# The first chunk's attention in plain float32 products over its three key blocks

## The chip, the cores and the metric

One core of a Trainium2 chip runs the kernel. The time is the device time of one execution in microseconds. The kernel before was timed three times: 816.13, 816.46 and 816.73 us, median 816.46 us. One further execution was profiled; it took 815.83 us, of which 814.1 us lie between its first and its last instruction (the span).

## The reference

Attention with a few sink keys and a sliding window, then a two-layer network on the concatenated heads. The shapes are batch 4, 8 heads, 768 positions, head size 64; 4 sinks, window 128; model width 512, hidden width 2048; all float32.

```python
scores = scale * np.matmul(q, k.transpose(0, 1, 3, 2))
keep = is_sink | in_window
scores = np.where(keep, scores, -1000000000.0)
scores = scores - np.max(scores, axis=-1, keepdims=True)
a = np.exp(scores)
a = a / (np.sum(a, axis=-1, keepdims=True) + 1e-09)
x = np.matmul(a, v)          # then heads side by side: 3072 x 512
h = x @ w_in
r = np.maximum(h, 0.0)
out = (s * (r * r) + b) @ w_out
```

## The kernel before, in words

**Chunks.** The 3072 rows are cut into eight chunks of 384 rows (half a sequence). A chunk has an attention part and a network part (`moe_steps`). The attention of chunk 0 runs by itself at the start; from then on the network steps of chunk c are issued together with the attention slots of chunk c+1. The instructions of each engine then run in a fixed order that the scheduling framework wrote when the kernel was built; an instruction whose operand is late holds up everything behind it on its engine.

**High and low parts.** TensorE is fed with float32r operands, a rounded form of float32. To keep precision, an operand is split into a high part (its rounded value) and a low part (what is left), and a product is made of two or three products of parts that add up in PSUM. Making parts is work for ScalarE (the rounding copy), VectorE and GpSimd (the subtraction).

**Attention, a head at a time, three units of 128 rows (i = 0, 1, 2).** `prep_head` (L225 to L239) splits queries, keys and values. `unit_a` multiplies queries with 144 or 272 keys (the 16 first keys as sinks, and the one or two blocks of 128 keys that the window reaches) in two products (L253, L254), applies the mask and the row maximum on VectorE in one instruction (L258, tile sm), takes the exponential on ScalarE (L264), and copies the sink columns aside on GpSimd (L265). `unit_b` transposes the block or two blocks on TensorE (L273, L275) and splits the result (L277 on ScalarE, L278 on VectorE, tile hl). `unit_c` multiplies with the values (L302). The row sums are collected in zz, and their reciprocal and the sinks' share are applied once for a pair of heads through further small products (L314, L325, L327; L284 to L288, L328 to L331).

**Weights.** Both weight matrices are cut into 32 pieces of 128x512, 8 bytes for a value (they come as float64). `load_piece` fetches a piece raw (512 KB) into the buffer w{p+2} of 32 named buffers w0 to w31, the last two pieces elsewhere. `make_piece` turns it into high and low parts: two ScalarE passes (L160, L161), two VectorE passes (L162, tile wt; L163, tile wraw), one GpSimd add (L165), two steps later a ScalarE rounding copy (L169), another two steps later the low part (L174, on VectorE for three pieces in four, otherwise on GpSimd), into buffer w{p}. Network step f of the first chunk needs pieces 2f and 2f+1; they are kept for the other seven chunks.

**Network.** `l1(f)` makes 12 products 128x384 (L379), Relu on ScalarE (L382), r on VectorE (L383), g high on ScalarE (L385), g low on VectorE (L386). `l2(f)` makes 9 products 128x512 (L397). There are 16 steps f in a chunk.

**The two stages of the start.** The text calls *first stage* the time up to the first L383 of chunk 0, and *second stage* the time from there to the fourteenth L383 of chunk 0; by then all pieces but a last one have been through VectorE.

## Time and profile before

| | |
|---|---|
| median of three runs | 816.46 us |
| the profiled execution | 815.83 us, span 814.1 us |
| TensorE matmul busy | 767.5 us, 94% of the span |
| VectorE (DVE) busy | 534.5 us, 66% |
| ScalarE (ACT) busy | 517.2 us, 64% |
| GpSimd (POOL) busy | 294.1 us, 36% |
| mean granted TensorE clock | 0.952 of full speed |

TensorE is the busiest engine over the whole, but not everywhere: a view that cuts the span into stretches shows which engine has no idle time in each. A row of such a view gives the stretch, then for each engine the busy time and, in brackets, the number of instructions, then the granted clock, the share of the DMA engines and their rate. In a timeline, a row gives the start, the duration, the engine, the line, the operation and its tiles, and in square brackets the idle time before it and what ended it. In a view of groups, a row gives the line, the engine, the operation, its tiles and shapes, the count, then busy us and the mean in ns, then the idle time before.

### The profile page before, as it was taken

What the parts mean: (1) busy time and instruction counts of PE and PEld (TensorE: products, weight loads), DVE (VectorE), ACT (ScalarE), POOL (GpSimd) and SP (SyncE); (2) the same over time, 40 slices, a digit from 0 to 9 for tenths busy, and PEclk for the clock granted to TensorE, in tenths of its full rate; (3) what the DMA queues carried; (4) which work ended last, traced back from release to release, by engine and by line L of the source; (5) the groups of instructions that cost most, each with busy time, mean ns of one, the idle gap of its engine ahead of it and who ended that gap; (6) DMA issues with size and microseconds to landing.
All of it is one profiled execution on the core that took longest, in us unless ns stands there. A gap on an engine that the chain in (4) does not pass through costs nothing.

```text
span 814.1 us, 12959 instructions
## 1 busy us (share of the span) xinstructions
PE 767.5 (94%) x4304; PEld 698.8 (86%) x4304; DVE 534.5 (66%) x1301; ACT 517.2 (64%) x1306; POOL 294.1 (36%) x473
## 2 busy tenths in 40 slices
...
GB/s 205 223 260 286 111 29 38 46 67 73 47 49 41 56 77 41 65 45 52 52 44 54 69 52 50 55 43 52 52 45 54 74 54 47 28 1 39 1 0 43
DMA packets 31754, 55.44 MB, mean 68 GB/s; under 512 B 4032, under 2 KB 18368, under 8 KB 31680
## 3 DMA queue, kind: packets, MB, share of 16 engines
...
## 4 chain that ended last, share of the span: by engine, by line
PE 79%; DVE 12%; ACT 3%; issue 2%; POOL 1%; DMA 1%; SPq 0%; POOLq 0%; ACTq 0%; DVEq 0%
PE h L379 31%; PE po L397 30%; PE o L302 7%; PE sc L254 3%; PE sc L253 2%; PE tp L273 2%; DVE wt L162 2%; PE tp L275 2%; DVE wraw L163 2%; DVE r L383 2%; DVE sm L258 1%; PE ts L314 1%; DVE w L174 1%; DVE g L386 1%; PE os L325 1%
## 5 line engine op out<-in xcount | busy, mean ns | idle before, releaser
L379 PE MATMUL h<-x,w 128*128 128x384 f32 x1536 | 303.9, 348 | 8.6 <-DVE negm L258 5.4
L397 PE MATMUL po<-w,g 128*128 128x512 f32 x1152 | 294.7, 400 | 1.4 <-DVE g L386 1.4
L379 PEld LDWEIGHTS h<-x,w 128*128 128x128 f32 x1536 | 274.2, 193 | 13.4 <-DVE negm L258 6.8
L397 PEld LDWEIGHTS po<-w,g 128*128 128x128 f32 x1152 | 209.1, 188 | 42.7 <-DVE g L386 1.8
L258 DVE CUSTOM_DVE_ANT_0 sm<-sc,msk 128x272 f32<-128x272 f32 (+1 forms) x192 | 79.8, 416 | 103.2 <-PE sc L254 75.0
L265 POOL COPY psk<-sm 128x48 f32<-128x48 f32 x192 | 56.7, 296 | 226.2 <-ACT sm L264 225.4
L382 ACT ACTIVATE r<-h 128x384 f32<-128x384 f32 x128 | 63.0, 492 | 115.5 <-PE h L379 114.4
L302 PE MATMUL o<-hl,vv 128*128 128x128 f32 x704 | 124.3, 296 | 2.7 <-DVE hl L278 2.5
L383 DVE SCALAR_TENSOR_TENSOR r<-r,sb 128x384 f32<-128x384 f32 x128 | 83.6, 654 | 56.3 <-ACT r L382 56.3
L264 ACT ACTIVATE sm<-sm,negm 128x272 f32<-128x272 f32 (+1 forms) x192 | 97.2, 506 | 29.3 <-DVE negm L258 28.2
L386 DVE SCALAR_TENSOR_TENSOR g<-r,sb,g 128x384 fp32r<-128x384 f32 x128 | 83.7, 655 | 44.3 <-ACT g L385 41.8
L302 PEld LDWEIGHTS o<-hl,vv 128*128 128x128 f32 x704 | 104.1, 206 | 4.7 <-DVE hl L278 3.8
L233 POOL TENSOR_TENSOR kl<-kraw,kh 128x416 fp32r<-128x416 f32 (+1 forms) x64 | 81.8, 1278 | 54.2 <-ACT kh L231 53.0
L385 ACT ACTIVATE g<-r,sb 128x384 fp32r<-128x384 f32 x128 | 78.8, 616 | 35.0 <-DVE r L383 33.0
L277 ACT CAST hl<-tp 128x256 fp32r<-128x256 f32 (+1 forms) x192 | 67.2, 351 | 33.5 <-PE tp L275 32.5
L278 DVE TENSOR_TENSOR hl<-tp,hl 128x256 fp32r<-128x256 f32 (+1 forms) x192 | 76.0, 397 | 10.8 <-ACT hl L277 7.9
L238 POOL TENSOR_TENSOR vv<-vraw,vv 128x192 fp32r<-128x192 f32 (+1 forms) x64 | 46.4, 726 | 77.6 <-ACT vv L237 77.2
L273 PE MATMUL tp<-identr,sm 128*128 128x128 f32 x192 | 56.5, 295 | 10.0 <-ACT sm L264 5.7
L253 PE MATMUL sc<-kh,qs 128*128 128x272 f32 (+1 forms) x192 | 58.4, 306 | 5.7 <-ACT kh L231 3.4
L254 PE MATMUL sc<-kl,qs 128*128 128x272 f32 (+1 forms) x192 | 58.4, 306 | 3.6 <-POOL kl L233 3.5
L310 DVE TENSOR_TENSOR xm<-o,y 64x384 f32<-64x384 f32 x64 | 35.4, 553 | 24.9 <-ACT y L309 24.5
L232 DVE TENSOR_TENSOR qs<-qraw,qs 64x384 fp32r<-64x384 f32 x64 | 43.5, 680 | 8.0 <-ACT qs L228 5.9
...
## 6 DMA issues: line engine op xcount, KB each, us to landing
wraw<-in_w SPq DMA_DIRECT2D x32, 512.0 KB, 5.6
...
```

What stands on the lines that cost most here:

```text
L233: nc.gpsimd.tensor_tensor(out=hd.kl[:, :kw], in0=hd.k[:, :kw], in1=hd.kh[:, :kw].bitcast(F32), op=ALU.subtract)
L253: nc.tensor.matmul(sc[:, :n], hd.qs[:, qs], hd.kh[:, c0:c0 + n], start=True, stop=False)
L254: nc.tensor.matmul(sc[:, :n], hd.qs[:, qs], hd.kl[:, c0:c0 + n], start=False, stop=True)
L258: nc.vector.tensor_tensor_reduce(out=sm[:, :n], in0=sc[:, :n], in1=m, scale=-0.125, scalar=BIG, op0=ALU.add, op1=ALU.min, accum_out=negm[: ...
L264: nc.scalar.activation(sm[:, :n], sm[:, :n], AF.Exp, bias=negm[:, uu], scale=-1.0, accum_out=pp.zz[:, i, hh:hh + 1])
L278: nc.vector.tensor_tensor(out=hl[:, 1, :n], in0=tp[:, :n], in1=hl[:, 0, :n].bitcast(F32), op=ALU.subtract)
L302: nc.tensor.matmul(hd.o[:, qs], hd.vv[:, cur - j, :], hl[:, t, j * P:(j + 1) * P], start=((j, t) == mm[0]), stop=((j, t) == mm[-1]))
L379: nc.tensor.matmul(h[:, :CH], pieces[2 * f][:, wi, cc * P:(cc + 1) * P], x[xi][:, cc, :], start=(i == 0), stop=(i == 11))
L383: nc.vector.scalar_tensor_tensor(out=r, in0=r, scalar=s_ap, in1=r, op0=ALU.mult, op1=ALU.mult)
L385: nc.scalar.activation(gg[:, 0, :], r, AF.Identity, bias=b_ap, scale=1.0)
L386: nc.vector.scalar_tensor_tensor(out=gg[:, 1, :], in0=r, scalar=b_ap, in1=gg[:, 0, :].bitcast(F32), op0=ALU.add, op1=ALU.subtract)
L397: nc.tensor.matmul(po[tb], gg[:, gi, tsl], pieces[2 * f + 1][:, wi, :], start=(f == 0 and i == 0), stop=(f == NF - 1 and i == 2))
```

## The change

For chunk 0 alone, the attention slots come from a new function, `first_slots`.

- No parts are made of queries, keys, values or weights of the attention. A product of float32 operands is asked of TensorE directly. Queries of a pair of heads are loaded into a buffer whose other 64 partitions are set to zero, so that one product works on 128 partitions.
- Unit i multiplies with all i+1 key blocks up to its own (128, 256 or 384 keys), under full masks that hold window and sinks together (`m_full`, six blocks of 128 made in `constants`). The sinks need no path of their own: no copies to psk, no sink products, no row-sum products for the pair.
- The row sum is inverted for each unit and applied on VectorE to the exponentials (three small or middle VectorE instructions), before the transposes.
- Transposes are 1, 2 and 3 blocks; the copy out of PSUM is on ScalarE for i = 0 and 1 and on VectorE for i = 2. The three units of a head share three products with the values, of 384, 256 and 128 columns, once for a head.
- The result's high part is taken on ScalarE, its low part on VectorE (on GpSimd before).
- Buffers: queries, keys and values of the four pairs lie in w16 to w23, the transposed exponentials in w24 to w27, the scores in two buffers w28 and w29, the masks in w30 (warm was and is in w31). A raw piece p goes into w{p+2}: pieces 14 to 28 find their buffer used by the first chunk's attention.
- All loads of chunk 0, 28 transfers, are asked for ahead of the first piece of the weights.

The attention of chunks 1 to 7, the network and the preparation of a piece are not edited.

```diff
--- before.py
+++ after.py
@@ -57,6 +57,18 @@
     msk = const.tile([P, 3 * W + P + NS], MDT, tag="msk", name="msk")
     m_1, m_odd, m_even = (msk[:, j * W:(j + 1) * W] for j in range(3))
     m_0 = msk[:, 3 * W:]
+
+
+    def late(j, shape, dtype, name):
+        n = 1
+        for x in shape[1:]:
+            n *= x
+        t = const.tile([P, 2 * DM], F32, tag=f"w{j}", name=name)
+        t = t if dtype is F32 else t.bitcast(dtype)
+        return t
+
+    m_all = late(2 * NF - 2, [P], MDT, "m_all")
+    m_full = [m_all[:, a * P:(a + j + 1) * P] for j, a in ((0, 0), (1, 1), (2, 3))]
 
 
 
@@ -110,7 +122,7 @@
 
 
         nc.vector.scalar_tensor_tensor(out=low, in0=rel, scalar=w_ap, in1=low, op0=ALU.is_lt, op1=ALU.mult)
-        nc.vector.tensor_scalar(out=snk[:, :NS], in0=kix[:, :NS], scalar1=n_ap, scalar2=None, op0=ALU.is_lt)
+        nc.vector.tensor_scalar(out=snk, in0=kix, scalar1=n_ap, scalar2=None, op0=ALU.is_lt)
         nc.vector.tensor_tensor(out=tmp[:, :NS], in0=low[:, :NS], in1=snk[:, :NS], op=ALU.mult)
         nc.vector.tensor_tensor(out=tmp[:, :NS], in0=snk[:, :NS], in1=tmp[:, :NS], op=ALU.subtract)
 
@@ -127,6 +139,19 @@
         mask(m_1[:, P:2 * P], low)
         mask(m_1[:, 2 * P:], tm2[:, :NS])
         mask(m_even[:, P:P + NS], snk[:, :NS])
+
+        for j in range(BLK):
+            mj = m_full[j]
+            for kb in range(j + 1):
+                keep = low if kb == j else upp if kb == j - 1 else None
+                if kb > 0:
+                    kept = keep
+                elif keep is None:
+                    kept = snk
+                else:
+                    kept = (tmp, tm2)[j]
+                    nc.vector.tensor_tensor(out=kept, in0=keep, in1=snk, op=ALU.max)
+                mask(mj[:, kb * P:(kb + 1) * P], kept)
         cp = nc.gpsimd.tensor_copy
         cp(out=m_even[:, :P], in_=m_1[:, :P])
         cp(out=m_even[:, P + NS:], in_=m_1[:, P:2 * P])
@@ -345,13 +370,8 @@
         def slot(t):
             def f():
 
-                for j, (fn, a) in enumerate(ahead.get(t, ())):
+                for fn, a in ahead.get(t, ()):
                     fn(k, a)
-                    if k.c == 0 and t == 0 and j == 0:
-                        constants()
-                if k.c == 0 and t == 0:
-                    nc.sync.dma_start(sb[:, 0:1], s.partition_broadcast(P))
-                    nc.sync.dma_start(sb[:, 1:2], b.partition_broadcast(P))
                 if t < n:
                     unit_a(k, *units[t])
                 if 0 <= t - LB < n:
@@ -363,6 +383,94 @@
             return f
 
         return k, [slot(t) for t in range(n + LC + LD)]
+
+
+    def first_slots():
+        k = new_chunk(0)
+        F0 = 2 * NF - 16
+        cc, tt, hd_o = {}, {}, {}
+
+        def load(pr):
+            pp = k.pairs[pr] = Chunk()
+            qk = const.tile([P, 2, DM], F32, tag=f"w{F0 + 2 * pr}", name="q_0")
+            kv = const.tile([P, 2, DM], F32, tag=f"w{F0 + 2 * pr + 1}", name="kv_0")
+
+            nc.gpsimd.memset(qk[D:, 0, :CH], 0.0)
+            nc.gpsimd.memset(qk[:D, 1, :CH], 0.0)
+            for hh in range(2):
+                hs = slice(hh * D, (hh + 1) * D)
+                nc.sync.dma_start(qk[hs, hh, :CH], qT[0, pr, hs, :CH])
+                h = 2 * pr + hh
+                nc.sync.dma_start(kv[hs, 0, :2 * P], kT[0, h, hs, NS:NS + 2 * P])
+                nc.sync.dma_start(kv[hs, 0, 2 * P:CH], kT[0, h, hs, 2 * NS + 2 * P:2 * NS + 3 * P])
+            nc.sync.dma_start(kv[:, 1, :CH].rearrange("p (n e) -> p n e", n=BLK),
+                              v[0, pr, :, :BLK].rearrange("p n h d -> p n (h d)"))
+            pp.q, pp.k, pp.v = qk[:, :, :CH], kv[:, 0, :CH], kv[:, 1, :CH]
+
+        def fa(h, i):
+            pp = k.pairs[h // 2]
+            n = (i + 1) * P
+            u = h * BLK + i
+            uu = slice(u, u + 1)
+            sc = ps("sc0")
+            nc.tensor.matmul(sc[:, :n], pp.q[:, h % 2, i * P:(i + 1) * P], pp.k[:, :n], start=True, stop=True)
+            sm = const.tile([P, CH], F32, tag=f"w{F0 + 12 + u % 2}", name="sm0")
+            nc.vector.tensor_tensor_reduce(out=sm[:, :n], in0=sc[:, :n], in1=m_full[i], scale=-0.125, scalar=BIG,
+                                           op0=ALU.add, op1=ALU.min, accum_out=negm[:, uu])
+            z = wk.tile([P, 3], F32, name="z0", tag="zr", bufs=2)
+            nc.scalar.activation(sm[:, :n], sm[:, :n], AF.Exp, bias=negm[:, uu], scale=-1.0, accum_out=z[:, 0:1])
+            nc.vector.tensor_scalar(out=z[:, 1:2], in0=z[:, 0:1], scalar1=1e-9, scalar2=None, op0=ALU.add)
+            nc.vector.reciprocal(out=z[:, 2:3], in_=z[:, 1:2])
+            nc.vector.tensor_scalar(out=sm[:, :n], in0=sm[:, :n], scalar1=z[:, 2:3], scalar2=None, op0=ALU.mult)
+            cc[(h, i)] = sm
+
+        def fb(h, i):
+            sm = cc.pop((h, i))
+            if i == 0:
+                tt[h] = const.tile([P, 4, 2 * P], F32, tag=f"w{F0 + 8 + h % 4}", name="tt0")
+            tp = ps("tp0")
+            for kb in range(i + 1):
+                nc.tensor.transpose(tp[:, kb * P:(kb + 1) * P], sm[:, kb * P:(kb + 1) * P], ident)
+
+            t0, c0 = i // 2, i % 2 * P
+            out = tt[h][:, t0:t0 + i + 1, c0:c0 + P]
+            (nc.scalar.copy if i < 2 else nc.vector.tensor_copy)(out, tp[:, :(i + 1) * P].rearrange("p (k c) -> p k c", c=P))
+
+        def fc(h, i):
+            if i < BLK - 1:
+                return
+            pr, hs = h // 2, slice(h % 2 * D, (h % 2 + 1) * D)
+            pp = k.pairs[pr]
+            o = ps("o0")
+            t = tt.pop(h).rearrange("p k c -> p (k c)")
+            for kb in range(BLK):
+                c0 = kb * 3 * P
+                nc.tensor.matmul(o[:, kb * P:CH], pp.v[:, kb * P:(kb + 1) * P], t[:, c0:c0 + (BLK - kb) * P],
+                                 start=(kb == 0), stop=(kb == BLK - 1))
+            nc.scalar.copy(k.x[0][hs, pr, :], o[hs, :CH])
+            nc.vector.tensor_tensor(out=k.x[1][hs, pr, :], in0=o[hs, :CH], in1=k.x[0][hs, pr, :].bitcast(F32), op=ALU.subtract)
+
+        units = [(h, i) for h in range(H) for i in range(BLK)]
+        n = len(units)
+
+        def slot(t):
+            def f():
+                if t == 0:
+                    for pr in range(H // 2):
+                        load(pr)
+                        if pr == 0:
+                            constants()
+                    nc.sync.dma_start(sb[:, 0:1], s.partition_broadcast(P))
+                    nc.sync.dma_start(sb[:, 1:2], b.partition_broadcast(P))
+                if t < n:
+                    fa(*units[t])
+                if 0 <= t - 1 < n:
+                    fb(*units[t - 1])
+                if 0 <= t - 3 < n:
+                    fc(*units[t - 3])
+            return f
+
+        return k, [slot(t) for t in range(n + 3)]
 
 
     def moe_steps(x, store, wk, before=None, last=False):
@@ -508,7 +616,7 @@
         weights(2 * f + 3 + LOADS, 2 * f + 3)
 
     NC_ = 2 * B
-    k, slots = attn_slots(0)
+    k, slots = first_slots()
     for f in slots:
         f()
     one = const.tile([P, 1], F32, tag="one", name="one")
```

What the edits do to the order of the engines is seen at three places. A line number of the changed kernel differs from that of the kernel before: L383 (r) is L491 there, L162, L163 and L174 are L187, L188 and L199, L258 (sm) of later chunks is L283, L149 (the raw load) is L174.

**VectorE at the first r of the network.** Before (L162, L163, L174: the three passes of a piece; L329: the end of a pair's attention; L258 is already chunk 1):

```order
L329 TENSOR_TENSOR xm<-zb,xm 128x384
L258 ISA sm,negm<-sc,msk 128x272
L258 ISA negm 128x1
L232 TENSOR_TENSOR qs<-qraw,qs 64x384
L162 TENSOR_SCALAR wt<-wraw 128x512
L174 TENSOR_TENSOR w_981<-wraw,w_981 128x512
L163 SCALAR_TENSOR_TENSOR wraw<-wraw,wt 128x512
L162 TENSOR_SCALAR wt<-wraw 128x512
L258 ISA sm,negm<-sc,msk 128x272
L258 ISA negm 128x1
L383 SCALAR_TENSOR_TENSOR r<-r,sb 128x384 x2
```

After (L451: the low part of a head's attention result; L437: the copy of the transposed block for i = 2):

```order
L437 COPY tt_530<-tp_553 128x3x128
L199 TENSOR_TENSOR w_1149<-wraw,w_1149 128x512
L187 TENSOR_SCALAR wt<-wraw 128x512 x2
L188 SCALAR_TENSOR_TENSOR wraw<-wraw,wt 128x512 x2
L451 TENSOR_TENSOR x_0_97<-o_558,x_0_96 64x384
L199 TENSOR_TENSOR w_1242<-wraw,w_1242 128x512
L187 TENSOR_SCALAR wt<-wraw 128x512
L283 ISA sm,negm<-sc,msk 128x272
L283 ISA negm 128x1
L188 SCALAR_TENSOR_TENSOR wraw<-wraw,wt 128x512
L491 SCALAR_TENSOR_TENSOR r<-r,sb 128x384
```

Ahead of the first r there stood 10 instructions of L162, 9 of L163 and 6 of L174; now there stand 21, 21 and 13 of the same three passes. Up to the fourteenth r it was 32, 32 and 23, and is 32, 32 and 24: eleven pieces have moved from the second stage into the first.

**The queue of SyncE at its start.** Before (raw pieces in between the first loads; sb: the two scalars):

```order
L80 DMA lim<-in_n_sink 128x2
L81 DMA lim<-in_window 128x2
L195 DMA qraw<-in_qT 128x384
L197 DMA vraw<-in_v 128x384
L210 DMA kraw<-in_kT 128x416
L217 DMA vsraw<-in_vsk 128x128
L353 DMA sb<-in_s 128x1
L354 DMA sb<-in_b 128x1
L149 DMA wraw<-in_w 128x1024 x2
```

After (kv and q: keys, values and queries of the last pair of chunk 0):

```order
L404 DMA kv_184<-in_kT 64x256
L405 DMA kv_184<-in_kT 64x128
L406 DMA kv_184<-in_v 128x384
L463 DMA sb<-in_s 128x1
L464 DMA sb<-in_b 128x1
L174 DMA wraw<-in_w 128x1024 x11
L220 DMA qraw<-in_qT 128x384
```

Behind the two loads of lim (the limits), four loads and the two scalars stood ahead of the first raw piece; now all 28 loads of chunk 0 and the two scalars stand there, and then eleven pieces follow one upon the other.

**TensorE about the fourth head of chunk 0.** Before (two products of scores a unit, transposes, products with the values of 128 columns):

```order
L275 MATMUL tp<-identr,sm 128x128
L254 MATMUL sc<-kl,qs 128x144
L302 MATMUL o<-hl,vv 128x128 x2
L314 MATMUL ts<-identr,psk_89 128x128 x3
L253 MATMUL sc<-kh,qs 128x272
L254 MATMUL sc<-kl,qs 128x272
L273 MATMUL tp<-identr,sm 128x128
L275 MATMUL tp<-identr,sm 128x128
L302 MATMUL o<-hl,vv 128x128 x6
L325 MATMUL os<-xsk,vs 128x384
L327 MATMUL zb<-xsk,sel 128x384
L253 MATMUL sc<-kh,qs 128x272
```

After:

```order
L416 MATMUL sc_323<-kv_162,q_161 128x128
L433 MATMUL tp_332<-identr,sm_306 128x128 x3
L416 MATMUL sc_337<-kv_162,q_161 128x256
L433 MATMUL tp_347<-identr,sm_325 128x128
L416 MATMUL sc_350<-kv_162,q_161 128x384
L433 MATMUL tp_359<-identr,sm_339 128x128 x2
L448 MATMUL o_363<-tt_300,kv_162 128x384
L448 MATMUL o_363<-tt_300,kv_162 128x256
L448 MATMUL o_363<-tt_300,kv_162 128x128
L416 MATMUL sc_369<-kv_173,q_172 128x128
L433 MATMUL tp_378<-identr,sm_352 128x128 x3
```

A head had 6 products of scores, 5 transposes and 10 products with the values, and for a pair of heads 5 more; now it has 3, 6 and 3, with operands in plain float32, and the three products of one head with the values stand together, ahead of the next head's third group of transposes.

## The prediction

> **What bounds the kernel now.** The first view cuts the span into three stretches: up to the first r, from there to the fourteenth, and about a chunk's length after that.
>
> ```profile
> core 0: us, PE busy (x) PEld busy (x) DVE busy (x) ACT busy (x) POOL busy (x), PEclk, DMA share, GB/s
> 0.00:75.00 75.00, 56.38 (x236) 47.42 (x237) 58.62 (x172) 59.23 (x157) 47.58 (x85) 0.64 0.72 235
> 75.00:176.00 101.00, 80.13 (x415) 70.98 (x414) 97.04 (x181) 82.80 (x189) 67.72 (x71) 0.90 0.24 77
> 182.00:272.00 90.00, 89.95 (x531) 82.84 (x530) 59.45 (x156) 58.44 (x158) 29.23 (x55) 1.00 0.18 51
> ```
>
> From 182 us TensorE has no idle time and its full clock; the edit touches nothing there. In the second stage VectorE is busy for 97.04 of 101 us (96%): it sets the pace. In the first stage nothing is full (VectorE 78%, ScalarE 79%, TensorE 75% at a granted clock of 0.64): the engines wait for one another. The stages' ends are read in VectorE's timeline (the middle row is an r that nothing held up).
>
> ```profile
> 74.94 2.62 DVE L383 SCALAR_TENSOR_TENSOR r<-r,sb 128x384 f32<-128x384 f32 x2
> 79.95 0.61 DVE L383 SCALAR_TENSOR_TENSOR r<-r,sb 128x384 f32<-128x384 f32 x1
> 176.11 0.92 DVE L383 SCALAR_TENSOR_TENSOR r<-r,sb 128x384 f32<-128x384 f32 x1
> ```
>
> What fills VectorE is read in its groups, first those of the second stage:
>
> ```profile
> L163 DVE SCALAR_TENSOR_TENSOR wraw<-wraw,wt 128x512 int32<-128x512 int32 x23 | 19.7, 856 | 0.2
> L162 DVE TENSOR_SCALAR wt<-wraw 128x512 int32<-128x512 int32 x22 | 15.2, 691 | 1.4 <-ACT wraw L161 1.4
> L174 DVE TENSOR_TENSOR w<-wraw,w 128x512 fp32r<-128x512 f32 x17 | 12.4, 728 | 0.0
> L386 DVE SCALAR_TENSOR_TENSOR g<-r,sb,g 128x384 fp32r<-128x384 f32 x12 | 12.2, 1024 | 0.1
> L383 DVE SCALAR_TENSOR_TENSOR r<-r,sb 128x384 f32<-128x384 f32 x13 | 12.1, 935 | 0.0
> ```
>
> Nearly half of the stage, 47.3 us, is the preparation of weights (first three rows). So the time is set by how much VectorE work lies ahead of the fourteenth r, plus VectorE's idle time up to there. At that point the old and the new order stand equal (all pieces through), and I take the rest as unchanged. The change in time is then that of the first stage plus that of the second.
>
> **Second stage.** By the order, 11 of L162, 12 of L163 and 6 of L174 leave it. Recorded durations overlap by some 0.07 us (below, the 0.43 us row at 12.91 is followed at 13.27), so what leaves is 11 x 0.62 + 12 x 0.79 + 6 x 0.66 = 20.2 us of 97.0. A dozen GpSimd adds leave too, and with them a part of what VectorE waits for GpSimd: r lasts 0.935 us here on the mean and 0.61 undisturbed, g's low part (L386, the same shape) 1.024: 9 us of excess in the two rows. GpSimd's 67.72 us fall by some 13, a fifth, so 2 us. Left: 74.8 us, at 96% 78 us. TensorE comes close: its 415 matmuls would take 415/531 x 90 = 70 us at the pace of the third stretch, at this stage's clock of 0.90 78 us. Two engines near their limit in fixed orders also wait for each other: I take 80 us, **21 us less**. Bounds: 78 us (VectorE alone) and 88 us (each adds 10 us of waits to TensorE's 78).
>
> **First stage, its start.** The rows of the constants, of SyncE's first issues and of the first landing:
>
> ```profile
> 0.75 0.39 SPq L80 DMA_DIRECT2D lim<-in_n_sink  x1
> 4.50 0.91 SPq L149 DMA_DIRECT2D wraw<-in_w  x2
> 6.50 0.16 DVE L515 TENSOR_SCALAR one<-wp 128x1 f32<-128x1 f32 x1
> 9.09 0.52 DVE L99 TENSOR_SCALAR sc<-sc 128x128 f32<-128x128 f32 x1
> 10.07 0.21 DVE L101 TENSOR_SCALAR sc<-sc 128x128 f32<-128x128 f32 x1
> 11.28 0.68 ACT L160 ACTIVATE wraw<-wraw 128x512 int32<-128x512 uint32 x1 [2.77 <-DMA wraw<-in_w]
> 12.05 0.72 DVE L119 TENSOR_SCALAR msk<-sc 128x16 bf16<-128x16 f32 x5
> 12.69 0.30 DVE L258 CUSTOM_DVE_ANT_0 sm<-sc,msk 128x144 f32<-128x144 f32 x1
> 12.91 0.43 DVE L258 CUSTOM_DVE_ANT_0 sm<-sc,msk 128x272 f32<-128x272 f32 x1
> 13.27 0.43 DVE L258 CUSTOM_DVE_ANT_0 sm<-sc,msk 128x272 f32<-128x272 f32 x1
> 14.09 0.53 ACT L264 ACTIVATE sm<-sm,negm 128x272 f32<-128x272 f32 x1
> ```
>
> The masks no longer queue behind a split of queries, so they start at 6.6 in place of 9.09, take the 3.6 us of before and 1.4 us more (six blocks at 0.13, two maxima at 0.23 like the sm of 144 columns, a wider comparison): the first scores are masked at 11.5 us. Eight issues took 3.75 us, so 32 ahead of the first piece take 15 us: it is asked for at 15.8 in place of 4.50. The median landing of a piece takes 5.6 us:
>
> ```profile
> wraw<-in_w SPq DMA_DIRECT2D x32, 512.0 KB, 5.6
> ```
>
> With two ScalarE passes at 0.55 start to start VectorE gets it at 22.5 us. Until then it has only units: a pair of units, with two score buffers, costs 0.7 for sm, 1.0 for two exponentials, some 0.5 for the three new VectorE steps, 0.8 for transposes and the next scores, 3 us; six units, 9 us, bring it to 20.5. So nothing is lost by the late start that the units don't fill, but 2 us; a raw piece later than 22.5 costs its lateness.
>
> **First stage, the rest.** From 22.5 us the order gives VectorE 18 units, 21 pieces through L162 and L163, 13 through L174, two splits of queries and one sm of chunk 1. The prices:
>
> ```profile
> L163 DVE SCALAR_TENSOR_TENSOR wraw<-wraw,wt 128x512 int32<-128x512 int32 x9 | 8.2, 907 | 0.1
> L232 DVE TENSOR_TENSOR qs<-qraw,qs 64x384 fp32r<-64x384 f32 x10 | 6.9, 694 | 2.8 <-ACT qs L228 2.3
> L162 DVE TENSOR_SCALAR wt<-wraw 128x512 int32<-128x512 int32 x10 | 5.5, 558 | 0.1
> L310 DVE TENSOR_TENSOR xm<-o,y 64x384 f32<-64x384 f32 x8 | 4.4, 552 | 0.3
> L174 DVE TENSOR_TENSOR w<-wraw,w 128x512 fp32r<-128x512 f32 x6 | 4.1, 684 | 0.0
> L328 DVE TENSOR_TENSOR xm<-os,xm 128x384 f32<-128x384 f32 x4 | 2.2, 558 | 1.3 <-PE os L325 1.3
> L285 DVE RECIPROCAL zr<-zr 128x6 f32<-128x6 f32 x4 | 0.7, 185 | 0.1
> 54.63 0.42 DVE L162 TENSOR_SCALAR wt<-wraw 128x512 int32<-128x512 int32 x1
> ```
>
> Pieces, each less 0.07: 21 x (0.49 + 0.84) + 13 x 0.61 = 35.8 us. A head: sm of 128, 256 and 384 columns by the rows of 144 and 272, 0.21 + 0.34 + 0.47; three additions like L515, 0.27; three reciprocals, 0.35; the scaling, 0.21 us at 128 columns (L101) and 0.42 at 512 (L162 undisturbed), so 0.14 + 0.21 + 0.28; the copy of 384 columns out of PSUM like L328, 0.49; the low part like L310, 0.48. That is 3.24 us, six heads 19.4 us. The rest 1.6 us. Sum 56.8 us.
>
> The new additions and scalings are of L162's kind, which GpSimd holds up: 0.558 us on the mean here and 0.42 undisturbed. At 0.14 us each, 36 of them cost 5.0 us; the bounds are nothing and the rival below. With 61.8 us of work VectorE runs at 78% (the first stage so far) to 96% (the second). I take 94%, near the second, because pieces now stand between the units in its queue: 65.7 us. The first r comes at 88.2 us, **13.2 us later** than at 75. Bounds: 56.8/0.96, first r at 81.7 (6.7 later); 61.8/0.78, at 101.7 (26.7 later).
>
> **TensorE in the first stage.** How long a plain float32 product streams, no row shows; the last product of the kernel is one, with a single column:
>
> ```profile
> L538 PEld LDWEIGHTS cnt<-one,bad x2: 79/80/82, 807.4 to 807.4; 128*1 128x1 f32 x2
> L538 PE MATMUL cnt<-one,bad x2: 163/164/164, 807.4 to 807.4; 128*1 128x1 f32 x2
> 25.22 0.52 PE L253 MATMUL sc<-kh,qs 128*128 128x272 f32 x1
> 25.54 0.43 PE L254 MATMUL sc<-kl,qs 128*128 128x272 f32 x1
> 25.77 0.41 PE L273 MATMUL tp<-identr,sm 128*128 128x128 f32 x1
> 25.98 0.42 PE L275 MATMUL tp<-identr,sm 128*128 128x128 f32 x1
> ```
>
> It is recorded as two weight loads and two matmuls. So the low bound is two passes; the high bound is four, since two operands of two parts have four products of parts. A head has 2 x (128 + 256 + 384) = 1536 columns of products. At half clock 272 columns take 0.23 us (25.54 to 25.77), new weights 0.09 more, a transpose 0.21: two passes give 2.6 + 1.1 + 1.3 = 5.0 us a head, four 7.6; eight heads 40 or 61 us. I take four. From 11.5 us that ends at 73, and copy, low part, twelve products of h and Relu add some 6: 79 us, short of VectorE's 88. VectorE is the cover for these 21 us; without it they would lie on the path.
>
> The Trainium skill (FP8 and Floating Point Precision, TensorE Precision Notes) says that true float32 takes four passes through the array; by it the head costs the 7.6 us, and the sum stays.
>
> **The rivals.** *More is won.* GpSimd loses the splits of keys and values and the sink copies of chunk 0, so it may hold up nothing: both low bounds, 6.7 - 23 = -16 us, 800 us. Against it: the exposed instructions have grown in number.
>
> *TensorE takes the second stage over.* 88 us there, 13.2 - 13 = 0, 816 us. For it: the two engines' sums are equal, 78 us.
>
> *GpSimd's adds hold VectorE up in full* (the side of slower). Every L163 releases an add on GpSimd, and what follows it on VectorE now is mostly of the exposed kind.
>
> ```profile
> L165 POOL TENSOR_TENSOR wraw<-wraw 128x512 int32<-128x512 int32 x7 | 7.6, 1085 | 2.9 <-DVE wraw L163 2.9
> L286 DVE CAST zh<-zr x7: 163/514/1037, 23.9 to 154.2; 128x6 fp32r<-128x6 f32 x7
> ```
>
> A copy of six elements took 163 ns alone and 1037 at worst. If each of 21 adds blocks VectorE for its 1.085 us, that is 22.8 us where I have counted 8 (5.0 and the 0.14 in L162): 15 us more, -8 + 15 = +7, 823 us. It decides from 0.37 us an add on beyond what is counted. Against it: L162 itself lost only 0.14.
>
> The Trainium skill (SBUF — State Buffer, SBUF: two separate sides) says that the port pair which the two engines share is an exclusive lock, held for a whole instruction, which is this rival; the 1037 ns agree with it, the mean of L162 shows it seldom in full.
>
> *TensorE at half clock, unit after unit.* If it stands still while a pair of units is exponentiated and scaled (1.7 us, twelve pairs, 20 us) and the clock stays at 0.5, the first stage is 11.5 + 61 + 20 + 6 = 99 us, 24 - 21 = +3, 819 us. For it: the granted clock was 0.64 in that stage. Against it: four-pass products keep TensorE denser than now.
>
> **How the numbers follow.** Forecast: 13.2 - 21 = -7.8 us on the profiled execution's own 815.83, 808.0; the median of the runs is 0.6 higher, so 808.7. Chances: the forecast (803 to 814) 0.44, more won 0.17, TensorE in the second stage 0.11, GpSimd 0.15, half clock 0.13. The range, 799 to 822, takes in the forecast, the second stage's rival and half clock, and about half of each of the other two, whose own spread goes some us to either side: 0.16 is left out. What this kernel's measurement can tell from no change is about 0.2%, 1.6 us: faster 0.41 + 0.17 + 0.04 = 0.62, same 0.08, slower 0.30.
>
> **What would show it.** Right: r number one at 82 to 93 us, number fourteen 77 to 84 us later; VectorE over 90% busy from 22 us on; each plain product as two matmuls, columns at a quarter of float32r's rate; the first piece at VectorE near 22 us. Wrong: long idle rows on VectorE ended by TensorE or by a weight transfer in the first stage; additions and scalings of over 0.5 us on the mean (GpSimd); a granted clock of 0.5 all through; a second stage above 88 us with VectorE below 90%.

## The result and the profile after

The changed kernel takes 827.01 us (median of four runs, 826.80 to 827.62), the kernel before, timed beside it, 816.56 us (816.13 to 816.73). The ratio is 1.0135, with an interval of 1.0123 to 1.0148: slower by 10.5 us, where 8 us faster was forecast. The profiled execution has a span of 825.8 us.

The loss is all made by the sixteenth r of chunk 0. From the start of that r to the end of the span it is 625.9 us before (814.1 - 188.23) and 625.3 us after (825.8 - 200.55); in all kernels of this study it lies between 624.2 and 626.5 us. So a kernel's time here is the moment of its sixteenth r and a nearly constant rest.

First the stretches of the kernel before, cut at 25.75 us, the first, the eighth and the sixteenth r, and at last the whole up to the sixteenth (columns as in the prediction's first fence):

```profile
0.00:25.75 25.75, 13.70 (x48) 8.54 (x49) 17.73 (x58) 16.62 (x42) 16.11 (x36) 0.73 0.61 205
25.75:74.94 49.19, 42.63 (x188) 38.82 (x188) 40.84 (x116) 42.55 (x115) 31.41 (x49) 0.59 0.77 251
74.94:123.50 48.56, 37.97 (x198) 33.67 (x197) 45.68 (x86) 39.62 (x93) 32.29 (x35) 0.89 0.31 104
123.50:188.23 64.73, 54.01 (x288) 47.92 (x287) 61.17 (x119) 51.18 (x118) 44.11 (x46) 0.92 0.17 54
0.00:188.23 188.23, 148.31 (x717) 128.95 (x718) 165.41 (x373) 149.97 (x365) 123.92 (x165) 0.80 0.43 139
```

The same stretches of the changed kernel:

```profile
0.00:25.75 25.75, 15.79 (x48) 8.92 (x48) 11.90 (x64) 7.39 (x21) 7.60 (x25) 0.73 0.52 141
25.75:97.77 72.02, 44.05 (x135) 28.36 (x136) 65.71 (x165) 56.29 (x129) 36.47 (x31) 0.67 0.66 228
97.77:148.03 50.26, 39.48 (x198) 33.68 (x198) 46.35 (x87) 36.43 (x86) 30.95 (x32) 0.86 0.10 29
148.03:200.55 52.52, 49.19 (x294) 44.87 (x294) 37.16 (x91) 34.67 (x89) 21.32 (x33) 1.00 0.24 70
0.00:200.55 200.55, 148.52 (x672) 115.82 (x673) 161.12 (x401) 134.78 (x321) 96.34 (x121) 0.81 0.39 126
```

Up to the sixteenth r VectorE works 161.1 us where it worked 165.4, 4.3 us less, and is idle 39.4 us where it was idle 22.8. Stretch by stretch its idle time changes by +5.8 (8.0 to 13.9, the start), -2.0, +1.0 and +11.8 us (3.6 to 15.4, from the eighth to the sixteenth r). In that last stretch TensorE is busy 49.19 of 52.52 us at full clock: there it is the limit, and VectorE has run out of work.

In VectorE's timeline the ends of the two stages, the first and the fourteenth r:

```profile
97.77 0.61 DVE L491 SCALAR_TENSOR_TENSOR r<-r,sb 128x384 f32<-128x384 f32 x1
189.09 0.62 DVE L491 SCALAR_TENSOR_TENSOR r<-r,sb 128x384 f32<-128x384 f32 x1
```

The first stage takes 22.8 us more (forecast 13.2), the second 91.3 us in place of 101.2, 9.9 less (forecast 21). VectorE's groups between 25.75 and 97.77 us:

```profile
L188 DVE SCALAR_TENSOR_TENSOR wraw<-wraw,wt 128x512 int32<-128x512 int32 x21 | 17.3, 829 | 0.0
L187 DVE TENSOR_SCALAR wt<-wraw 128x512 int32<-128x512 int32 x21 | 12.3, 595 | 4.3 <-ACT wraw L186 4.3
L199 DVE TENSOR_TENSOR w<-wraw,w 128x512 fp32r<-128x512 f32 x13 | 12.1, 931 | 0.0
L424 DVE TENSOR_SCALAR sm<-sm,z 128x128 f32<-128x128 f32 (+2 forms) x18 | 9.9, 552 | 0.0
...
L422 DVE TENSOR_SCALAR z<-z 128x1 f32<-128x1 f32 x18 | 2.6, 145 | 1.2 <-ACT sm L421 1.0
```

The first three rows are weight preparation, 41.7 of 65.7 us. With VectorE at 91% of this stretch, the first stage looks like VectorE's. The experiments show that the amount of its work is not what sets the pace.

### The profile page after: what moved, and what is told of

Same layout as the page of the kernel before. It is cut to its first block, busy times and chain, and to the rows that moved or that the text cites. A ratio compares the mean times of both kernels' runs of the same rounds, so it can differ in the third digit from the quotient of the medians.

```text
span 825.8 us, 12816 instructions
## 1 busy us (share of the span) xinstructions
PE 767.0 (93%) x4260; PEld 685.6 (83%) x4260; DVE 530.5 (64%) x1329; ACT 500.6 (61%) x1262; POOL 267.2 (32%) x429
## 4 chain that ended last, share of the span: by engine, by line
PE 81%; DVE 9%; ACT 3%; SPq 2%; issue 2%; DMA 2%; POOL 1%; POOLq 0%; DVEq 0%; ACTq 0%
PE h L487 31%; PE po L505 30%; PE o L327 7%; PE sc L279 2%; PE sc L278 2%; PE tp L298 2%; PE o L448 2%; PE tp L300 2%; DMA wraw<-in_w 2%; DVE w L199 1%; DVE wt L187 1%; DVE wraw L188 1%; PE ts L339 1%; DVE sm L424 1%; PE os L350 1%
## 5 line engine op out<-in xcount | busy, mean ns | idle before, releaser
L283 DVE CUSTOM_DVE_ANT_0 sm<-sc,msk 128x272 f32<-128x272 f32 (+1 forms) x168 | 70.6, 420 | 101.9 <-PE sc L279 75.4
L491 DVE SCALAR_TENSOR_TENSOR r<-r,sb 128x384 f32<-128x384 f32 x128 | 81.7, 638 | 60.6 <-ACT r L490 60.6
L327 PE MATMUL o<-hl,vv 128*128 128x128 f32 x624 | 101.3, 282 | 2.1 <-DVE xm L335 1.1
L289 ACT ACTIVATE sm<-sm,negm 128x272 f32<-128x272 f32 (+1 forms) x168 | 85.3, 508 | 26.4 <-DVE negm L283 25.4
L258 POOL TENSOR_TENSOR kl<-kraw,kh 128x544 fp32r<-128x544 f32 (+1 forms) x56 | 70.7, 1263 | 53.0 <-ACT kh L256 53.0
L327 PEld LDWEIGHTS o<-hl,vv 128*128 128x128 f32 x624 | 83.8, 191 | 3.4 <-DVE xm L335 1.6
L303 DVE TENSOR_TENSOR hl<-tp,hl 128x256 fp32r<-128x256 f32 (+1 forms) x168 | 67.3, 400 | 10.4 <-ACT hl L302 7.7
L263 POOL TENSOR_TENSOR vv<-vraw,vv 128x256 fp32r<-128x256 f32 (+1 forms) x56 | 38.5, 687 | 86.0 <-ACT vv L262 83.9
L190 POOL TENSOR_TENSOR wraw<-wraw 128x512 int32<-128x512 int32 x32 | 38.6, 1211 | 53.9 <-ACT wraw L185 17.4
L278 PE MATMUL sc<-kh,qs 128*128 128x272 f32 (+1 forms) x168 | 47.3, 281 | 2.2 <-DVE hl L303 1.5
L279 PE MATMUL sc<-kl,qs 128*128 128x272 f32 (+1 forms) x168 | 48.3, 287 | 0.0
L298 PE MATMUL tp<-identr,sm 128*128 128x128 f32 x168 | 46.2, 275 | 2.1 <-DVE negm L283 1.0
```

Source lines behind the costliest of these rows:

```text
L258: nc.gpsimd.tensor_tensor(out=hd.kl[:, :kw], in0=hd.k[:, :kw], in1=hd.kh[:, :kw].bitcast(F32), op=ALU.subtract)
L278: nc.tensor.matmul(sc[:, :n], hd.qs[:, qs], hd.kh[:, c0:c0 + n], start=True, stop=False)
L279: nc.tensor.matmul(sc[:, :n], hd.qs[:, qs], hd.kl[:, c0:c0 + n], start=False, stop=True)
L283: nc.vector.tensor_tensor_reduce(out=sm[:, :n], in0=sc[:, :n], in1=m, scale=-0.125, scalar=BIG, op0=ALU.add, op1=ALU.min, accum_out=negm[: ...
L289: nc.scalar.activation(sm[:, :n], sm[:, :n], AF.Exp, bias=negm[:, uu], scale=-1.0, accum_out=pp.zz[:, i, hh:hh + 1])
L303: nc.vector.tensor_tensor(out=hl[:, 1, :n], in0=tp[:, :n], in1=hl[:, 0, :n].bitcast(F32), op=ALU.subtract)
```

## The experiments

Each kernel below is the changed kernel with the edit shown, unless it says otherwise. "Head spacing" is the time from the second to the eighth reduction of 384 columns (one for each head of chunk 0), divided by six. The kernel before, timed beside them, took 814.7 to 817.0 us, and the four timings of e14 lie between 805.2 and 807.9. Of the kernels with an edit only e14 and e15 were timed more than once, so a difference of 2 to 3 us between two of them is not clear of noise.

| kernel | us | head spacing | first r | sixteenth r | pieces through L188 before the first r |
|---|---|---|---|---|---|
| before | 816.6 | | 74.9 | 188.2 | 9 |
| changed | 827.0 | 10.8 | 97.8 | 200.6 | 21 |
| e1 early raw pieces | 821.8 | 9.1 | 95.6 | 195.4 | 21 |
| e2 one pass | 818.2 | 8.7 | 81.6 | 191.2 | 15 |
| e3 no add | 814.0 | 10.1 | 92.3 | 187.4 | 21 |
| e4 no add, kernel before | 806.2 | | 72.7 | 178.5 | 9 |
| e5 pieces held back | 836.4 | 10.4 | 91.6 | 209.6 | 10 |
| e6 e5 + scaling on ScalarE | 820.7 | 7.7 | 75.3 | 191.9 | 10 |
| e7 four score buffers | 827.1 | 10.5 | 97.4 | 199.7 | 21 |
| e8 e5 + early | 832.0 | 7.9 | 91.2 | 205.7 | 10 |
| e9 one unit further ahead | 817.8 | 7.7 | 76.9 | 191.0 | 12 |
| e10 e9 + early | 815.1 | 7.2 | 82.1 | 188.5 | 17 |
| e11 e10 + scaling on ScalarE | 808.6 | 4.9 | 65.1 | 182.1 | 9 |
| e12 early + scaling on ScalarE | 819.6 | 7.9 | 86.6 | 193.0 | 17 |
| e13 e9 + one pass | 811.4 | 5.8 | 63.9 | 184.6 | 7 |
| e14 e11, timed four times | 806.4 | 5.2 | 65.3 | 179.6 | 9 |
| e15 e14 + copies on ScalarE | 811.1 | 4.7 | 59.5 | 182.3 | 7 |

Two things have to be kept in mind with this table. An edit also changes the order that the framework writes, and with it how many pieces stand between the heads (the last column shows a part of it). And in the kernels with early raw pieces (e1, e8, e10, e11, e12, e14, e15) the second reduction is itself late, at 21 to 31 us against 15 to 21 us in the others, so the spacing leaves out what was lost before it.

### Three suspects: late weights, four passes, GpSimd's adds

The changed kernel asks for its first raw piece only after 30 transfers of the first chunk, and VectorE gets it at 25.75 us (forecast 22.5):

```profile
19.58 0.43 SPq L464 DMA_DIRECT2D sb<-in_b  x1
20.05 0.91 SPq L174 DMA_DIRECT2D wraw<-in_w  x2
...
25.75 0.43 DVE L187 TENSOR_SCALAR wt<-wraw 128x512 int32<-128x512 int32 x1 [4.26 <-ACT wraw L186]
```

**e1.** The first ten raw pieces go between these transfers.

```diff
                         load(pr)
+                        while loaded[0] < (4, 6, 8, 10)[pr]:
+                            load_piece(loaded[0])
+                            loaded[0] += 1
```

> The changed kernel, with ten raw pieces asked for in between the loads of chunk 0 (four behind the first pair's loads, two behind each further pair's) in place of behind all 28 of them. In the changed kernel VectorE got its first piece at 25.75 us, the first r came at 97.8 us and the kernel took 827 us. Theory W (VectorE's work with its idle start sets the first stage): the first piece is at VectorE near 15 us, VectorE fills most of its 10 us of idle time between 12 and 26 us, the first r comes 7 to 10 us earlier, and the kernel is 5 to 10 us faster, 817 to 822 us. Theory T (TensorE at half clock and two score buffers set the first stage): the first r moves by less than 3 us, 824 to 827 us.

It took 821.8 us, 5.2 less: half of the loss, as expected of late weights. But the first r moved by 2.2 us only, where 7 to 10 were expected. The early pieces also hold the heads up: on ScalarE the first two exponentials now stand behind the first passes of three raw pieces and start at 15.0 us, though their reductions end by 12.0, and the second head's reduction comes at 29.0 us (19.3 in the changed kernel).

**e2.** The plain products read the upper 16 bits of their operands as bfloat16, in one pass.

```diff
-sc[:, :n], pp.q[:, h % 2, i * P:(i + 1) * P], pp.k[:, :n]
+sc[:, :n], pp.q16[:, h % 2, 2 * i * P + 1:2 * (i + 1) * P:2], pp.k16[:, 1:2 * n:2]
-o[:, kb * P:CH], pp.v[:, kb * P:(kb + 1) * P], t[:, c0:...]
+o[:, kb * P:CH], pp.v16[:, 2 * kb * P + 1:2 * (kb + 1) * P:2], t16[:, 2 * c0 + 1:...:2]
```

> The changed kernel, but each plain float32 product of chunk 0 reads only the upper 16 bits of both operands as bfloat16, so that it is one pass and not the reference's precision; nothing else is left out. TensorE's 2.57 us for a head's three value products become about 0.7 us. Theory W: TensorE had slack, the first r comes at most 3 us earlier than 97.8, 824 to 827 us. Theory T: TensorE's passes are on the path, the first r comes 10 to 20 us earlier, 808 to 817 us.

818.2 us, 8.8 less, between the two theories; the first r came 16.1 us earlier, as theory T has it. In TensorE's timeline the three products with the values (768 columns), in the changed kernel and then in this one:

```profile
44.35 2.77 PE L448 MATMUL o<-tt,kv 128*128 128x384 f32 x6
46.91 0.63 PE L416 MATMUL sc<-kv,q 128*128 128x128 f32 x2
```
```profile
45.47 0.84 PE L448 MATMUL o<-tt,kv 128*128 128x384 bf16 x3
```

Six recorded matmuls in place of three, and 2.56 us up to the next start in place of some 0.8; the granted clock is 0.50 in both places. So the passes do cost, though VectorE was 91% busy beside them.

**e3, e4.** GpSimd's add of a piece's low word is left out, in the changed kernel and in the kernel before.

```diff
-            nc.gpsimd.tensor_tensor(out=hi, in0=hi, in1=lo, op=ALU.add)
```

> The changed kernel without GpSimd's add in the preparation of a piece (32 adds of 1.2 us left out, so the weights lack their lowest part). In the changed kernel between 25.75 and 97.8 us VectorE's durations exceed their undisturbed ones by 13.5 us (scalings 0.552 for 0.35, the three passes of a piece 0.595 for 0.42, 0.829 for 0.69, 0.931 for 0.68). Theory G (GpSimd's adds hold VectorE up): these means fall to within 0.1 us of the undisturbed ones, the first r comes 8 to 13 us earlier, and the kernel is 12 to 20 us faster. Theory W without G: the means stay, the first r moves by under 3 us.

> The control for the run without adds: the kernel before, also without GpSimd's 32 adds. If the adds cost both kernels alike, it is faster than before by as much as the changed kernel is without them (12 to 20 us by theory G). If they explain why the change lost, it gains less than half of that.

The adds cost 13.1 us in the changed kernel and 9.9 us in the kernel before (816.04 to 806.18). Both pay, so only 3.2 us of the loss can be theirs. The first r came 5.5 us earlier, less than the 8 to 13 of theory G. How the payment looks, VectorE's first pass of a piece up to the sixteenth r, in the changed kernel and without the add:

```profile
L187 DVE TENSOR_SCALAR wt<-wraw 128x512 int32<-128x512 int32 x32 | 19.2, 609 | 7.3 <-ACT wraw L186 7.2
```
```profile
L187 DVE TENSOR_SCALAR wt<-wraw 128x512 int32<-128x512 int32 x32 | 14.3, 454 | 7.4 <-ACT wraw L186 7.3
```

The instruction itself gets longer, 0.61 us in place of 0.45; no wait is recorded for it.

### Too many pieces early, or the attention's own chain?

In the changed kernel 30 of 32 pieces are through VectorE's passes by the seventh r. Theory B: VectorE's part and then TensorE's part follow each other because the pieces come in a bunch. The experiment holds VectorE's instructions of a piece behind an earlier r, on VectorE's queue alone (`last_r[f - 3]` is the r of three steps before; `issue_after` sets the order of issue, and no wait).

```diff
     def before(f):
-        weights(2 * f + 3 + LOADS, 2 * f + 3)
+        if f < 3:
+            weights(2 * f + 3 + LOADS, 2 * f + 3)
+        else:
+            with tc.issue_after(last_r[f - 3]):
+                weights(2 * f + 3 + LOADS, 2 * f + 3)
```

> The changed kernel, with one thing altered: VectorE may begin its share of a weight piece only after the r of the feed-forward block three before the one that asks for the piece, so that it makes about 10 pieces before the first r of the first chunk (21 in the changed kernel, 10 in the kernel before) and then two for each r, as the kernel before does. Theory B: in the changed kernel VectorE makes 21 of 32 pieces before the first r and 30 by the seventh, so that TensorE starves up to the eighth r (VectorE's part) and VectorE idles from there to the sixteenth (TensorE's part, 15.4 of 52.5 us idle); the two parts add instead of lying beside each other. Spread out, some 11 pieces x 1.43 us and 7 subtractions x 0.93 us (22 us) leave the first stage: the first r moves from 97.8 to 75 to 82 us, the sixteenth from 200.6 to 185 to 192 (VectorE 161 us busy at 95% from the start, the late beginning of 10 us with it), and the time is 811 to 818. Rival N: the first chunk's attention is held by its own chain (four passes at half clock, two score buffers, three VectorE operations between the exponential and the transposes), and the pieces merely fill VectorE's gaps there: the first r stays at 90 or later, the sixteenth r comes later than 200, and the time is 825 to 840.

> As e5_spread, and besides the scaling of the probabilities runs on ScalarE and the addition of 1e-9 to the sums is left out (each sum holds a term that is 1, so a float32 sum does not change by it): VectorE loses 24 additions of 0.146 us and 24 scalings of 0.50 to 0.55 us, some 16 us, and ScalarE gains 24 scalings. Theory B with VectorE as the limit right up to the sixteenth r: 8 to 14 us below e5_spread (800 to 808). If instead TensorE is the limit once the pieces are spread: at most 4 us below e5_spread. If ScalarE becomes the limit of the first stage (56 of 72 us busy there in the changed kernel): no better than e5_spread, or worse.

> The changed kernel with four score buffers in place of two for the first chunk (they share the four of the later chunks, made 384 wide), nothing else. Theory Q: the 33.7 us for which the transposes wait for the scaled probabilities come from having two buffers only; with four the first r comes 5 to 10 us earlier and the time is 817 to 822. Theory B: VectorE is 91% busy in that stage and its work is the same, so the wait only moves: within 2.5 us of 827.

> As e5_spread, and ten raw pieces are asked for between the first chunk's own loads, as in e1_early (which gained 5.2 us on the changed kernel, 2.2 of it up to the first r). Theory B: with 10 pieces wanted before the first r in place of 21 the late first raw piece (25.8 us) is worth less, since VectorE has attention work by then: 1 to 4 us below e5_spread. Rival: VectorE's idle start (13.9 of the first 25.8 us, against 8.0 in the kernel before) is lost whatever follows, because VectorE is the limit to the sixteenth r: again 5 us or more below e5_spread.

**e5** went the other way: 836.4 us, first r at 91.6, sixteenth at 209.6. Rival N had all three numbers. The second and the eighth 384-column reduction of the changed kernel, then of e5, in VectorE's timeline:

```profile
19.28 0.56 DVE L418 CUSTOM_DVE_ANT_0 sm<-sc,m_all 128x384 f32<-128x384 f32 x1 [1.06 <-PE sc L416]
83.95 0.56 DVE L418 CUSTOM_DVE_ANT_0 sm<-sc,m_all 128x384 f32<-128x384 f32 x1 [0.23 <-PE sc L416]
```
```profile
19.93 0.56 DVE L419 CUSTOM_DVE_ANT_0 sm<-sc,m_all 128x384 f32<-128x384 f32 x1 [0.86 <-PE sc L417]
82.33 0.56 DVE L419 CUSTOM_DVE_ANT_0 sm<-sc,m_all 128x384 f32<-128x384 f32 x1 [0.56 <-PE sc L417]
```

The rows from 25 to 75 us, of the changed kernel and of e5:

```profile
25.00:75.00 50.00, 27.90 (x76) 16.61 (x75) 44.58 (x118) 38.83 (x93) 24.98 (x23) 0.63 0.66 235
```
```profile
25.00:75.00 50.00, 27.59 (x77) 16.91 (x78) 39.08 (x111) 38.52 (x92) 21.34 (x19) 0.62 0.65 234
```

VectorE has 5.5 us less to do in these 50 us, and the heads come almost as far apart, 10.4 us against 10.8. Between the two reductions shown it is busy for 54.9 of 64.7 us in the changed kernel and for 44.7 of 62.4 us in e5, where no engine is over 73%. So the amount of VectorE's work does not pace the heads; most of its pieces lay in gaps. Holding them back left the gaps empty, and the work came later. The hold is on VectorE alone: ScalarE does its first pass of a piece 18 times between these reductions in both kernels (11.8 and 12.0 us).

**e7** changes nothing (827.1): with four buffers the heads stay 10.5 us apart, so theory Q is out. **e8** gains 4.4 us on e5, a little over what theory B allowed. Its heads are 7.9 us apart although its ring is closed as in e5, but they begin 11.3 us later (second reduction at 31.2 us, eighth at 78.8), and ScalarE and VectorE have made more of their pieces by then. **e6**, with the scaling of the probabilities on ScalarE,

```diff
-nc.vector.tensor_scalar(out=z[:, 1:2], in0=z[:, 0:1], scalar1=1e-9, scalar2=None, op0=ALU.add)
-nc.vector.reciprocal(out=z[:, 2:3], in_=z[:, 1:2])
-nc.vector.tensor_scalar(out=sm[:, :n], in0=sm[:, :n], scalar1=z[:, 2:3], scalar2=None, op0=ALU.mult)
+nc.vector.reciprocal(out=z[:, 2:3], in_=z[:, 0:1])
+nc.scalar.mul(sm[:, :n], sm[:, :n], z[:, 2:3])
```

gains 15.7 us on e5, more than the expected 8 to 14, and its heads come 7.7 us apart. Some 16 us of work leave VectorE, but in e5 it was only 72% busy between the heads, so work taken off does not explain a gain of that size there. It points to the place where the scaling stood. Here is that place in the changed kernel's timeline (t is a unit of 384 columns, t+1 the next head's first):

```profile
55.81 2.77 PE L448 MATMUL o<-tt,kv 128*128 128x384 f32 x6
55.84 0.61 ACT L421 ACTIVATE sm<-sm,negm 128x384 f32<-128x384 f32 x1 [0.41 <-DVE negm L418]
...
57.27 0.14 DVE L422 TENSOR_SCALAR z<-z 128x1 f32<-128x1 f32 x1
...
58.37 0.44 PE L416 MATMUL sc<-kv,q 128*128 128x128 f32 x2
...
58.85 0.29 DVE L418 CUSTOM_DVE_ANT_0 sm<-sc,m_all 128x128 f32<-128x128 f32 x1 [1.44 <-PE sc L416]
...
59.07 0.16 DVE L423 RECIPROCAL z<-z 128x1 f32<-128x1 f32 x1
59.14 1.22 DVE L199 TENSOR_TENSOR w<-wraw,w 128x512 fp32r<-128x512 f32 x1
...
60.29 0.41 DVE L424 TENSOR_SCALAR sm<-sm,z 128x384 f32<-128x384 f32 x1
...
60.84 0.52 PE L433 MATMUL tp<-identr,sm 128*128 128x128 f32 x3 [2.03 <-ACT w L194]
```

Unit t is exponentiated by 56.5 us. VectorE does its addition at 57.27, and then its next instruction is the reduction of t+1, which waits 1.44 us for the scores of t+1; these stand on TensorE behind the 2.77 us of products with the values. Only then come the reciprocal, a piece's subtraction and the scaling of t, which ends at 60.70, and at 60.84 the transposes, for which TensorE has stood still since the scores. (The row names ScalarE's copy L194 as the releaser, but the transposes read the scaled tile.) The next scores are queued behind these transposes. It is a closed ring: scores of t+1 (TensorE), reduction of t+1 and scaling of t (VectorE), transposes of t (TensorE), scores of t+2. Where the order is this one, what either engine takes, the other waits through, and so a pass, a piece that gets between or a hold-up by GpSimd can lie on it. In the changed kernel 14 of 23 scalings stand behind the next unit's reduction; in all of them the transposes stand behind the next unit's scores. This is read from the timeline; e9 tests it.

### Opening the ring

**e9.** The transposes come two units behind the scores, the products with the values four; there are four score buffers for it, and four for the sums.

```diff
-                if 0 <= t - 1 < n:
-                    fb(*units[t - 1])
-                if 0 <= t - 3 < n:
-                    fc(*units[t - 3])
+                if 0 <= t - 2 < n:
+                    fb(*units[t - 2])
+                if 0 <= t - 4 < n:
+                    fc(*units[t - 4])
```

> The changed kernel with the transposes of a unit traced two units behind its scores in place of one, and the product with the values four behind in place of three; for it, four score buffers in place of two (which alone changed nothing: e7_four_buffers) and four for the sums. Theory C, formed after e5_spread: the first chunk's attention is a closed ring. TensorE does the scores of unit t+1, then the transposes of unit t, and the scores of t+2 stand behind those; VectorE does the reduction of t+1 ahead of the scaling of t. So neither engine works beside the other, a head takes 10.9 us (reductions 10.7 to 11.7 us apart per head, the same with 10 or 21 pieces), about 8 us of it TensorE's own (at half clock, four passes) and 3 us waiting, and the pieces only fill VectorE's gaps. One unit further ahead opens the ring: 8 to 8.8 us a head, first r at 76 to 84 us (97.8 in the changed kernel), fewer pieces before it (12), the sixteenth r at 182 to 192 and the time 809 to 818. Rival V: VectorE, 91% busy in the first stage, is the limit after all: the heads stay 10 us or more apart, the first r comes earlier only by the pieces that the order moves behind it, as in e5_spread, and the time is 824 to 837.

817.8 us, 9.2 less than the changed kernel (the kernel before took 815.1 beside it). The first r at 76.9 and the sixteenth at 191.0 are as theory C has it, the heads, 7.7 us apart, a little closer than its 8 to 8.8; the time is at the upper end of its range. Rival V is out. Its second and eighth reduction in the timeline, and its row from 25 to 75 us:

```profile
16.58 0.55 DVE L418 CUSTOM_DVE_ANT_0 sm<-sc,m_all 128x384 f32<-128x384 f32 x1
62.78 0.55 DVE L418 CUSTOM_DVE_ANT_0 sm<-sc,m_all 128x384 f32<-128x384 f32 x1
```
```profile
25.00:75.00 50.00, 33.09 (x122) 23.56 (x123) 45.99 (x128) 41.00 (x100) 21.67 (x20) 0.80 0.70 246
```

VectorE is no less busy than in the changed kernel (45.99 us against 44.58), and TensorE does 122 matmuls in place of 76, at a granted clock of 0.80 in place of 0.63.

What came off the path is read from the chain of work that ended last, followed back from each step to what released it. Its shares between the second and the eighth reduction, in the changed kernel (64.67 us) and in e9 (46.20 us), as far as the view prints them:

```profile
by line: PE o L448 19.8%; DVE sm L424 10.8%; PE sc L416 9.1%; DMA wraw<-in_w 9.0%; issue 8.7%; PE tp L433 8.5%; DVE wraw L188 5.4%; DVE w L199 3.9%; DVE sm L418 3.3%; DVE wt L187 2.8%; ACT wraw L186 2.6%; ACT w L194 2.6%; ACT sm L421 2.3%;
```
```profile
by line: DVE sm L424 13.4%; PE o L448 9.7%; DMA wraw<-in_w 9.3%; DVE wt L187 8.5%; DVE sm L418 8.2%; issue 5.5%; DVE wraw L188 5.3%; DVE x L451 4.6%; DVE tt L437 4.4%; PE tp L433 4.4%; DVE w L199 4.3%; ACT sm L421 3.9%; PE sc L416 3.7%; DVE
```

TensorE's products and transposes of the first chunk (L448, L416, L433) make 37.4% of it in the changed kernel, 24.2 us, and 17.8% in e9, 8.2 us: 16 of the 18.5 us by which the six heads come sooner. VectorE's three passes of a piece have 12.1% in the changed kernel, 7.8 us, so a part of the pieces did stand on the path. One thing is not kept apart: the order of e9 also puts fewer pieces between the heads (ScalarE's first pass 10 times there, 18 in the changed kernel and in e5). How much of the gain is the lookahead by itself is not shown.

> As e9_one_more_ahead, and ten raw pieces asked for between the first chunk's own loads, as in e1_early; the order then has 17 pieces before the first r in place of 12. Theory C: in the open ring VectorE's early idle time can be filled with pieces, so this is 2 to 6 us below e9_one_more_ahead (805 to 814). If the start does not matter once the ring is open: within 2 us of it.

> As e10_ahead_early, and the scaling of the probabilities on ScalarE, without the addition of 1e-9, as in e6_spread_act (where the heads came 8 and later 6 us apart). Theory C: the ring is open already, so what is gained is VectorE's work alone (24 x about 0.65 us, 16 us) where VectorE is the limit up to the sixteenth r, less what ScalarE takes on: 3 to 10 us below e10_ahead_early (797 to 808). If ScalarE (56 of 72 us busy in the changed kernel's first stage, some 12 us more here) becomes the limit: not below e10_ahead_early.

> The changed kernel with the scaling on ScalarE, without the addition, and ten raw pieces early, the units one ahead as in the changed kernel. Theory C: what made the heads 8 us in e6_spread_act was that the scaling no longer stands behind the next unit's reduction on VectorE, so the ring is shorter by two hops; here too the heads come 7 to 8.5 us apart with 17 pieces before the first r, which is at 74 to 82, and the time is 804 to 814. Rival: e6_spread_act was quicker only because VectorE had less to do beside few pieces; with 17 pieces the heads are 9.5 us or more apart and the time is 816 to 822.

**e10** (the early raw pieces as well) took 815.1 us, 2.8 less than e9: as expected if the start counts in the open ring too, but hardly more than the noise of single timings. **e11** (the scaling on ScalarE as well) took 808.6 us, 6.5 less again, within the 3 to 10 expected. VectorE's work alone is not what changed: the first r comes 17 us earlier, with 9 pieces ahead of it in place of 17, and between the second and the eighth reduction ScalarE is now busy for 28.6 of 29.5 us. **e12** does this last edit and the early pieces with the ring closed: 819.6 us, only 2.2 less than e1. Its heads are 7.9 us apart, as theory C said, but e8 has this spacing with the scaling still on VectorE, so it decides nothing; the first r came at 86.6 and not by 82, and the time is what the rival gave. The second head's reduction stands at 28.5 us (19.3 in the changed kernel), though its queries and keys are asked for ahead of all raw pieces. Here too the exponentials of the first two units stand on ScalarE behind the first passes of three raw pieces. Their reductions end by 12.1 us, but ScalarE waits 3.5 us for the second and the third piece to land, and the exponentials start at 17.47 us. From 25.75 us to the first r ScalarE is then busy for 53.3 of 60.9 us (88%), VectorE for 41.4. The same edit, with early pieces, gains 6.5 us in the open ring; what it gains in the closed one, 2.2 us, is within the noise.

> As e9_one_more_ahead, with the scores' and values' products read as the upper 16 bits of their operands (bfloat16, one pass in place of four, as in e2_one_pass, which gained 8.8 us on the changed kernel): the low bits of these operands are left out. Theory C: in the closed ring each pass stood in line with VectorE's work; in the open ring TensorE's extra passes lie beside it, so they are worth less now: 2 to 5 us below e9_one_more_ahead (813 to 816). If TensorE itself is the limit of the first stage once the ring is open: 7 to 10 us below it (808 to 811), with the heads 6 us apart or less. If the four passes cost nothing once VectorE has work beside them, as the prediction had it: within 1.5 us of it.

> e11_ahead_early_act again, timed in rounds beside the kernel before: the computation is whole. From its one look (808.6 against 815.1): a ratio of 0.990 to 0.994.

> As e14_ahead_early_act, and the copy of each head's third transposes on ScalarE too (VectorE loses 8 x 0.55 us, ScalarE gains as many). VectorE the limit up to the sixteenth r, and ScalarE not: 2 to 5 us below e14_ahead_early_act. ScalarE the limit while the first chunk lasts (24.2 of 25 us busy from 25 to 50 us in e11_ahead_early_act): 0 to 4 us above it.

**e13** took 811.4 us: one pass in place of four is worth 6.4 us in the open ring and 8.8 in the closed one. That lies between the two cases put down for it; the spacing, 6 us or less, is what the second one said, in which TensorE is the limit. So the passes were not a matter of the ring alone, and theory C had them too low; what paces the heads at 5.8 us there is not settled.

**e14** is the best version: 806.4 us against 815.8, ratio 0.988, interval 0.986 to 0.990, a little better than the 0.990 to 0.994 expected, with the whole computation (the added 1e-9 aside, which does not change a float32 sum that holds a 1). Its row from 25 to 75 us shows TensorE at 187 matmuls and a clock of 0.93, VectorE with 11.6 us to spare, and ScalarE with 5.7:

```profile
25.00:75.00 50.00, 38.95 (x187) 30.19 (x187) 38.40 (x103) 44.26 (x117) 16.96 (x18) 0.93 0.73 254
```

**e15** moves one copy in three of the transposes from VectorE to ScalarE: ratio 0.9935 (0.991 to 0.996), 811.1 us, 4.7 above e14, outside both ranges put down for it. Its heads are the quickest of all (4.7 us) and its first r is the earliest, with ScalarE busy for 33.8 of 34.5 us from 25 us to it, but it loses the lead later: from its first to its sixteenth r VectorE is busy for 120.1 of 122.8 us (108.5 of 114.3 in e14). VectorE's second pass of a piece, up to the sixteenth r, in e14 and in e15:

```profile
L188 DVE SCALAR_TENSOR_TENSOR wraw<-wraw,wt 128x512 int32<-128x512 int32 x32 | 24.9, 779 | 0.4
```
```profile
L188 DVE SCALAR_TENSOR_TENSOR wraw<-wraw,wt 128x512 int32<-128x512 int32 x32 | 27.8, 871 | 0.5
```

With L187 (0.593 to 0.725 us on the mean) that is 7.1 us more for the same 64 instructions; the third pass, L199, gets shorter (0.982 to 0.844 us, 3.4 us less in all). Why the durations change was not tried; that they then meet GpSimd's instructions more often is an argument only.

## Why the prediction was wrong, by its own steps

The sum put the fourteenth r at 88.2 + 80 = 168.2 us; it came at 189.1. Of the 20.9 us between, 9.6 are the first stage's (3.3 a later first piece, 3.9 more VectorE work, 2.4 more idle time) and 11.3 the second stage's (1.0 more work, 10.3 more idle time). The largest single step that failed is the second stage's 80 us; under the first stage's smaller miss lies the wrong mechanism.

**"So the time is set by how much VectorE work lies ahead of the fourteenth r, plus VectorE's idle time up to there."** This holds, with the sixteenth r in its place. The work was nearly well sized: 61.8 us forecast from the first piece to the first r, 65.7 measured; 74.8 us forecast in the second stage, 75.8 measured. The idle time was not: 15.5 us in the second stage, where 5.2 were allowed.

**"I take 94%, near the second, because pieces now stand between the units in its queue."** This is the step whose mechanism failed in the first stage; that 91% came out, near the 94, is luck. VectorE was read as the bound and its pieces as cover for TensorE. The pieces were in the main filling: in e5 VectorE had less to do and the heads stayed 10.4 us apart. TensorE and VectorE took turns in the ring, 24.2 of 64.7 us of the chain being TensorE's, and the first r came at 97.8 us and not at 88.2.

**"VectorE is the cover for these 21 us."** Wrong with it. Four passes were right, and so was their size (about 2.6 us for 768 columns at half clock), but where the two engines take turns neither covers the other: one pass saved 8.8 us.

**The rival "half clock, unit after unit"**, at 0.13, had the right mechanism for the first stage, and its 99 us for it are nearly what was measured (97.8). That it fits so well is in part luck: the granted clock was 0.67 from 25.75 us to the first r and not 0.5, and part of the time went to the late first piece. It named the exponential and the scaling as the wait. It did not see that the scaling stood behind the next unit's scores. That order was there to be read before: on TensorE scores, transposes, scores; on VectorE, in most units, the next reduction ahead of the scaling.

**"Left: 74.8 us, at 96% 78 us ... I take 80 us."** The second stage took 91.3 us. Both engines' sums, 75.8 us and 77.2 us, would have fitted into 80. But they did not lie beside each other. Its first stretch, up to the eighth r, is the third row of the changed kernel's stretches above; its second is this:

```profile
148.03:189.09 41.06, 37.73 (x226) 34.31 (x226) 29.44 (x73) 28.12 (x72) 17.01 (x26) 1.00 0.24 73
```

To the eighth r VectorE is 92% busy and TensorE 79%, after it TensorE 92%, at full clock, and VectorE 72%. The two maxima, 46.4 and 37.7 us, add up to 84.1 of the 91.3 us; the larger of the two sums would be 77.2. This is read from the two rows and from no run that changes it alone: e5, made to test it by spreading the pieces, had a second stage of 103.9 us and a later sixteenth r. The rival "TensorE takes the second stage over" (88 us, 0.11) came nearest. Given the ring, e5 shows that the bunch of pieces ahead was still better than its own order.

**"Eight issues took 3.75 us, so 32 ahead of the first piece take 15 us"**, with 2 us lost by it. The 28 new loads went out 0.62 us apart on the mean, not 0.47 (rows at the end), so the piece came 3.3 us later than forecast. The late start cost 5.2 us (e1).

**GpSimd.** 8 us of hold-ups were counted, 5.0 of them for the additions and scalings, and the rival had 15 more. The additions kept 0.145 us and lost next to nothing; the scalings (0.55 us on the mean, about 0.35 undisturbed over the three widths), the low parts (0.93 against 0.68) and the two passes (0.60 and 0.83 against 0.42 and 0.69) lost 3.6, 3.3, 3.7 and 2.9 us, 13.5 in all. So its sign, scalings of over 0.5 us on the mean, came true. Yet the kernel before pays nearly as much (e3, e4: 13.1 and 9.9 us), so at most 3.2 of the 10.5 us by which the change is slower are this rival's.

**The Trainium skill's rules.** Four passes (FP8 and Floating Point Precision, TensorE Precision Notes): the trace agrees, with 2.56 us for 768 columns in float32 at the clock of 0.50: by the prediction's float32r row (272 columns in 0.23 us) one pass would take 0.65 us, a quarter. In bfloat16 they took some 0.8 us, new weights included. The exclusive lock (SBUF — State Buffer, SBUF: two separate sides): VectorE's first pass takes 0.61 us beside the adds and 0.45 without them, which agrees with a hold-up; a full one for each add is not what the mean shows.
